# One tile for each quarter of w_in and w_out, and no dummy matmuls, in a fused gated-attention and MoE kernel

## The chip, the core and the metric

The kernel runs on one core of a Trainium2 chip. The metric is the device time in microseconds. A core has a matrix engine (TensorE, PE in the profile; its weight loads are PEld), a vector engine (VectorE, DVE), a scalar engine with function tables (ScalarE, ACT), a general engine (GpSimd, POOL) and SyncE (SP), which here only starts transfers. SP, ACT and POOL can each start DMA transfers; a transfer started by an engine stands in that engine's own order of instructions. Each engine runs its instructions in order; between engines semaphores order the work.

## What is computed

Four inputs of shape (batch 4, heads 8, sequence 768, head size 48) go through a recurrent attention; the result, as 3072 tokens of 384 numbers, goes through one feed-forward layer with w_in (384 x 2048) and w_out (2048 x 384).

```python
f = 1.0 / (1.0 + np.exp(-f_logit))
for t in range(S):
    state = f[:, :, t, :, None] * state + einsum('bhd,bhe->bhde', k[:, :, t], v[:, :, t])
    y[:, :, t] = einsum('bhd,bhde->bhe', q[:, :, t], state)
x = y.transpose(0, 2, 1, 3).reshape(B * S, H * D)
h = x @ w_in
out = (h * np.cos(h)) @ w_out
```

## The kernel before

**Tiling.** The 3072 tokens are 24 chunks of 128 (`C`), six for each batch. `chunk_load` (L391 to 402) fetches f, k, q and v of a chunk, four transfers of 192 KB, into one of seven sets of buffers. Which engine starts each transfer is in `QUEUES`, with one letter for each of f, k, q, v: chunk 0 "SAAP", chunk 1 "SSSS", chunk 2 "SSSA", so that chunk 2's v is started by ACT. `decay_group` (L404) makes the decay factors on ACT (exponential L412, logarithm L415, then L437 after a matmul). `attend` (L445) scales q and k (L458), casts v on POOL (L463), transposes (L481 on TensorE with L487 as the copy out, or a transposing DMA), forms the masked scores (L500, L507), carries the state (L519, L534, L538), makes y (L551, L554, L561) and its transpose x (L572, L561, tiles xT).

`moe` (L582) works on units of 128 or 256 tokens (`UNITS`). A unit's first half goes over groups of a PSUM bank: 12 matmuls (six in units of 256 tokens) of x with w_in (L597), the cosine on ACT (L605), the product on DVE (L609, tiles gT). Each group reads one quarter (512 columns) of w_in, and takes every fourth column of it, starting at f0. The second half (L619) multiplies gT by w_out, four matmuls for each quarter of w_out; the result is copied out (L628 or L630) and stored by SP (L633).

**Weights.** `load_weights` (L367) issues eight transfers from POOL, one for each quarter of w_in and of w_out, 384 KB each as written. Before the change w_in is one tile of 3 x 2048 columns and w_out one tile of 16 x 384; a quarter is a cut of that tile. A quarter of w_in is three pieces of 512 columns, 2048 apart; a quarter of w_out is contiguous. `GATES` holds each transfer back until the v of a given chunk is cast: 1, 1, 0, 1 for w_in and 1, 2, 2, 1 for w_out. So the third quarter of w_in (gate 0) is issued first, and the two middle quarters of w_out wait for chunk 2's v.

**Order.** All work is first written as operations with a cost, a priority and their dependences. A planner (`Plan.run`, L141) places them one by one: for each engine it computes the earliest start of every ready operation, with the ends of what it depends on, a free buffer, a free PSUM bank and a model of two DMA queues; it takes the operation of highest priority among those that can start soon, and where an operation may run on several engines, the one that would end first. The priorities come from lists of numbers (`ATT`, `DEC`, `MM1`, `MM2`). The result is a fixed order of instructions for each engine. The planner keeps its dependences by quarter of the weights. The semaphores are put in afterwards by the framework, from the address ranges that instructions read and write in a tile.

**Dummy matmuls.** `WARM` = 75 operations (L351 to 356) of two 128x128 matmuls of the identity with itself, of the lowest priority and in a PSUM bank that nobody reads. They are the 150 matmuls of L354. The planner gives each one 220 ns (the first 16) or 112 ns of TensorE.

The counters on which a transfer's end is seen are dealt in turn, eight for the transfers of SP and ACT together; a transfer whose counter is still in use waits for the one that used it.

Of the kernel before, what the change touches and what calls it, by code (L numbers as in the profile page):

```python
# [10 lines left out]
BF16 = mybir.dt.bfloat16  # L11
# [238 lines left out]
def kernel(  # L250
# [15 lines left out]
    d_model, d_ff = moe_w_in.shape  # L266
    n_tokens = B * S
    KM = d_model // 128
    KF = d_ff // 128
# [15 lines left out]
    QK_DMA = [7, 10, 12, 13, 14, 15, 16, 17, 18, 19, 20, 21, 22, 23]  # L285
    X_DMA = [7, 8, 11, 12, 13, 14, 16, 18, 19, 20, 21, 22, 23]
    FAST = 10
    WARM = 75
    BUFS = {"ld": 7, "vb": 6, "sp": 6, "b": 6, "bi": 4, "qk": 5, "qkt": 6, "am": 6, "sz": 4, "y": 4, "st": 2, "co": 5, "ot": 5, "g": 6}
    CAPS = [6, 4, 3, 3, 3]  # L290

    cpool = ctx.enter_context(tc.tile_pool(name="const", bufs=1))
# [42 lines left out]
    poS = Banks(base, "po", CAPS[2], [moe_cap])  # L335
    paS = Banks(base, "pa", CAPS[3])
    miS = Banks(base, "mi", CAPS[4])
    w_in_bf = cpool.tile([128, KM, d_ff], BF16, name="w_in_bf")
    w_out_bf = cpool.tile([128, KF, d_model], BF16, name="w_out_bf")

    P = Plan()

# [7 lines left out]
    warm = Val(phS)  # L350
    for i in range(WARM):  # L351
        def idle(e):
            for _ in range(2):
                nc.tensor.matmul(warm.ap[:, 0:128], lhsT=ident, rhs=ident, start=True, stop=True)  # L354
# [6 lines left out]


    NW = d_ff // 512
    w_in_v = [Val(ap=w_in_bf[:, :, i * 512:(i + 1) * 512]) for i in range(NW)]
    w_out_v = [Val(ap=w_out_bf[:, i * 4:(i + 1) * 4, :]) for i in range(KF // 4)]

    def load_weights(part, i, prio):  # L367
        if part == 0:
# [213 lines left out]
    def moe(u, t0, T):  # L582

        n0 = t0 // C
        xs, gT = xT[n0:(t0 + T) // C], Val(gS)
        x = x_sb[t0 // TOK][:, :, t0 % TOK:t0 % TOK + T]
        G = 512 // T
        span = T / C
        for j in range(KF // G):
            ph, co = Val(phS), Val(coS)  # L590

            def g1(e, j=j, ph=ph):
                for g in range(G):

                    s0, f0 = divmod(j * G + g, 4)
                    for m in range(KM):
                        nc.tensor.matmul(ph.ap[:, g * T:(g + 1) * T],  # L597
                                         lhsT=w_in_bf[:, m, s0 * 512 + f0:(s0 + 1) * 512:4],
                                         rhs=x[:, m, :],
                                         start=(g == 0 and m == 0),  # L600
                                         stop=(g == G - 1 and m == KM - 1))
            pr = MM1[u] + n0 + 0.5 * span * j * G / KF
            P.op({"PE": G * 3 * (T / 2.4 + 2.0)}, g1, reads=xs + [w_in_v[j * G // 4]],
                 writes=[ph], prio=pr, lat=170.0)
            P.op({"ACT": 490.0}, lambda e, ph=ph, co=co: nc.scalar.activation(  # L605
                out=co.ap, in_=ph.ap, func=AF.Sin, bias=HALF_PI),
                reads=[ph], writes=[co], prio=pr, table="S")
            gv = gT.part(lambda a, j=j: a[:, j * G:(j + 1) * G, 0:T])
            P.op({"DVE": 605.0}, lambda e, ph=ph, co=co, gv=gv: nc.vector.tensor_mul(  # L609
                out=gv.ap, in0=ph.ap.rearrange("p (g t) -> p g t", t=T),  # L610
                in1=co.ap.rearrange("p (g t) -> p g t", t=T)),
                reads=[ph, co], writes=[gv], prio=pr)
        for i in range(T // 128):
            po, ot = Val(poS), Val(otS)
            pr = MM2[u] + n0 + 0.5 * span + 0.5 * i
            for s in range(4):
                def g2(e, i=i, s=s, po=po):
                    for j in range(4 * s, 4 * s + 4):
                        nc.tensor.matmul(po.ap[:, 0:d_model],  # L619
                                         lhsT=gT.ap[:, j, i * 128:(i + 1) * 128],  # L620
                                         rhs=w_out_bf[:, j, :], start=(j == 0), stop=(j == KF - 1))
                P.op({"PE": 4 * 162.5}, g2,
                     reads=[gT.parts[q] for q in range(4 * s // G, (4 * s + 3) // G + 1)] + [w_out_v[s]],
                     writes=[po], prio=pr, lat=170.0 if s == 3 else 0.0)

            def ev(e, po=po, ot=ot):
                if e == "ACT":
                    nc.scalar.copy(out=ot.ap, in_=po.ap[:, 0:d_model])  # L628
                else:
                    nc.vector.tensor_copy(out=ot.ap, in_=po.ap[:, 0:d_model])  # L630
            P.op({"ACT": 375.0, "DVE": 475.0}, ev, reads=[po], writes=[ot], prio=pr)
            r0 = t0 + i * 128
            P.op({"SP": 500.0}, lambda e, ot=ot, r0=r0: nc.sync.dma_start(  # L633
                out=out[r0:r0 + 128, :], in_=ot.ap), reads=[ot], prio=pr, lat=1800.0, dma=500.0)
# [61 lines left out]
```

## Time and profile before

| | |
|---|---|
| median of 4 runs | 202.65 us (202.13 to 203.97) |
| profiled execution | 202.52 us |
| its span, first to last instruction | 200.6 us |
| granted TensorE clock, mean | 0.955 |
| PE busy | 179.4 us (89%), 2175 matmuls |
| DVE busy | 135.2 us (67%) |
| ACT busy | 138.2 us (69%) |
| POOL busy | 64.6 us (32%) |
| matmuls of L597 (x by w_in) | 864, 71.3 us |
| matmuls of L619 (gT by w_out) | 384, 71.2 us |
| dummy matmuls, L354 | 150, 12.5 us, from 1.4 to 26.5 us |
| transfers | 32.04 MB, mean 160 GB/s |

The profile is of one execution. A busy TensorE is not one at its peak, since matmuls overlap. In a line of the timeline the columns are: start, duration, engine, line of the kernel, operation, output and inputs, number of instructions, and in brackets the idle time before and what ended it. A line of the chain of waits has start, duration and what the chain went through. "SPq", "ACTq" and "POOLq" are an engine's issuing of transfers.

### The profile page before, as it was taken

How to read it: one execution, taken by the hardware profiler on the slowest of the kernel's cores; microseconds unless marked ns; L12 is line 12 of the kernel's file. 1: busy time of each engine (PE TensorE's matmuls, PEld its weight loads, DVE VectorE, ACT ScalarE, POOL GpSimd, SP SyncE). 2: the span in 40 equal slices, each digit the busy share in tenths (PEclk: the TensorE clock that was granted, in tenths of full speed). 3: DMA queues.
4: the chain of work that ended last, by engine and by line, in shares of the span. 5: the costliest groups of instructions: out<-in, count | busy, mean ns of one | idle time of the engine just before them, and what ended most of it. 6: DMA issues, size and time to landing. Idle time of an engine off the chain costs nothing.

```text
span 200.6 us, 5468 instructions
## 1 busy us (share of the span) xinstructions
PE 179.4 (89%) x2175; PEld 143.3 (71%) x2175; DVE 135.2 (67%) x254; ACT 138.2 (69%) x250; POOL 64.6 (32%) x105
## 2 busy tenths in 40 slices
PE   6891498299999999999999999889999999999991
PEld 6791397278766967998668785778678768697770
DVE  7592049376599999899757985569617984691630
ACT  4473026648598999999797469964879979193451
POOL 7290000360040213551786223911059257000000
PEclk9998569859999999999999999999999999999998
DMA  7999999992199798997999997999799954603003
GB/s 139 215 192 195 203 184 205 188 169 52 40 192 196 132 199 189 213 188 150 189 196 164 176 185 191 234 167 193 141 223 208 221 154 114 159 16 98 3 0 119
DMA packets 124713, 32.04 MB, mean 160 GB/s; under 512 B 119520, under 2 KB 124128, under 8 KB 124688
## 3 DMA queue, kind: packets, MB, share of 16 engines
q1 hardware_dynamic: 117248, 27.37, 68.4%
q0 software_dynamic: 2240, 3.34, 9.5%
q10 hardware_dynamic: 5200, 0.98, 2.6%
q8 instruction: 17, 0.28, 0.6%
q14 instruction: 8, 0.07, 0.1%
HBM read 25.17 MB, written 4.72 MB: 149 GB/s over the span
## 4 chain that ended last, share of the span: by engine, by line
PE 53%; SPq 14%; DMA 13%; DVE 9%; ACT 4%; issue 3%; POOL 2%; ACTq 0%; POOLq 0%; DVEq 0%
PE ps L597 23%; PE ps L619 20%; SPq L399 14%; DMA v<-in_v_dram 6%; DMA qkt<-qk 5%; DMA xT<-y 3%; DVE gT L609 3%; PE ps L500 3%; DVE am L507 2%; POOL qk L458 2%; DVE qk L458 2%; PE ps L551 1%; PE ps L427 1%; PE ps L519 1%; ACT cosh L605 1%
## 5 line engine op out<-in xcount | busy, mean ns | idle before, releaser
L597 PE MATMUL ps<-xT,w_in_bf 128*128 128x128 bf16 (+1 forms) x864 | 71.3, 243 | 8.4 <-DMA w_in_bf<-in_moe_w_in_dram 7.3
L597 PEld LDWEIGHTS <-w_in_bf 128*128 128x128 bf16 x864 | 66.8, 116 | 11.2 <-issue 5.2
L605 ACT ACTIVATE cosh<-ps 128x512 bf16<-128x512 f32 x96 | 54.4, 603 | 25.5 <-PE ps L597 21.2
L609 DVE TENSOR_TENSOR gT<-ps,cosh 128x512 bf16<-128x512 f32 x96 | 61.3, 686 | 15.6 <-ACT cosh L605 15.3
L619 PE MATMUL ps<-w_out_bf,gT 128*128 128x384 bf16 x384 | 71.2, 326 | 0.0
L619 PEld LDWEIGHTS <-gT 128*128 128x128 bf16 x384 | 34.5, 98 | 19.3 <-DVE gT L609 0.2
L507 DVE TENSOR_TENSOR am<-ps,umask 128x512 bf16<-128x512 f32 x48 | 30.5, 685 | 3.9 <-PE ps L500 3.7
L463 POOL CAST vb<-v 128x384 bf16<-128x384 f32 x24 | 12.1, 506 | 62.0 <-DMA v<-in_v_dram 52.4
L538 POOL TENSOR_TENSOR sz<-st,b 64x192 bf16<-64x192 f32 x32 | 16.6, 520 | 39.0 <-DVE st L534 30.9
L437 ACT ACTIVATE b<-ps 128x388 f32<-128x388 f32 x24 | 11.9, 497 | 11.6 <-PE ps L430 9.4
L534 DVE TENSOR_TENSOR st<-ps,sz 64x192 f32<-64x192 f32 x32 | 11.3, 354 | 9.0 <-PE ps L519 6.9
L561 ACT CAST y<-ps 128x384 bf16<-128x384 f32 x19 | 9.2, 482 | 10.1 <-PE ps L554 9.2
L458 POOL TENSOR_TENSOR qk<-q,b 128x384 bf16<-128x384 f32 x14 | 14.1, 1005 | 3.2 <-ACT b L437 2.5
L458 POOL TENSOR_TENSOR qk<-k,bi 128x384 bf16<-128x384 f32 x14 | 14.0, 1002 | 0.2
L354 PE MATMUL ps<-ident 128*128 128x128 bf16 x150 | 12.5, 245 | 1.4 <-POOL ident masks.py:199 1.4
L487 DVE COPY qkt<-ps 128x512 bf16<-128x512 bf16 x15 | 6.2, 422 | 10.8 <-PE ps L481 10.7
L412 ACT ACTIVATE f<-f 128x384 f32<-128x384 f32 x24 | 12.5, 522 | 1.0 <-DMA f<-in_f_logit_dram 0.9
L415 ACT ACTIVATE sp<-f 128x384 bf16<-128x384 f32 x24 | 12.6, 524 | 0.8
L630 DVE COPY ot<-ps 128x384 f32<-128x384 f32 x9 | 5.0, 556 | 10.2 <-PE ps L619 8.3
L437 ACT ACTIVATE bi<-ps 128x384 f32<-128x384 f32 x24 | 11.9, 495 | 0.0
L354 PEld LDWEIGHTS <-ident 128*128 128x128 bf16 x150 | 10.7, 112 | 1.6 <-POOL ident masks.py:199 1.4
L605 ACT ACT_TABLE_LOAD x9 | 11.5, 1283 | 0.2
(42 smaller groups left out, 153.7 us busy)
## 6 DMA issues: line engine op xcount, KB each, us to landing
f<-in_f_logit_dram SPq DMA_DIRECT2D x24, 192.0 KB, 4.0
out_dram<-ot SPq DMA_DIRECT2D x24, 192.0 KB, 2.3
k<-in_k_dram SPq DMA_DIRECT2D x23, 192.0 KB, 4.0
q<-in_q_dram SPq DMA_DIRECT2D x22, 192.0 KB, 3.8
v<-in_v_dram SPq DMA_DIRECT2D x21, 192.0 KB, 4.0
w_in_bf<-in_moe_w_in_dram POOLq DMA_DIRECT2D x4, 384.0 KB, 8.6
w_out_bf<-in_moe_w_out_dram POOLq DMA_DIRECT2D x4, 384.0 KB, 9.3
q<-in_q_dram ACTq DMA_DIRECT2D x2, 192.0 KB, 4.0
```

The lines of the kernel that those rows point to most:

```text
L354: nc.tensor.matmul(warm.ap[:, 0:128], lhsT=ident, rhs=ident, start=True, stop=True)
L399: P.op(eng, lambda e, t=t, ap=ap, dma=dma: dma.dma_start(out=t.ap, in_=ap), writes=[t], prio=prio, lat=3000.0 if way == "P" else 1250.0, d ...
L412: nc.scalar.activation(out=f.ap, in_=f.ap, func=AF.Exp, scale=-1.0)
L415: nc.scalar.activation(out=sp.ap[:, :, 0:D], in_=f.ap, func=AF.Ln, bias=1.0)
L437: nc.scalar.activation(out=o.ap, in_=pc.ap[:, 0:n], func=AF.Exp, scale=s)
L458: lambda e, src=src, w=w, dst=dst: E(e).tensor_mul(out=dst.ap, in0=src.ap, in1=w.ap[:, 0:H * D].rearrange("p (h d) -> p h d", d=D)),
L507: nc.vector.tensor_mul(out=am.ap, in0=pa.ap.rearrange("p (a n) -> p a n", n=C), in1=umask[:, None, :].broadcast_to([128, 4, C]))
L538: o = P.op(cost, lambda e, g=g, srcap=srcap, out=out: E(e).tensor_mul(out=out.ap, in0=srcap(), in1=bt.ap[rows(g), H * D:, None].broadcast_ ...
L597: nc.tensor.matmul(ph.ap[:, g * T:(g + 1) * T], lhsT=w_in_bf[:, m, s0 * 512 + f0:(s0 + 1) * 512:4], rhs=x[:, m, :], start=(g == 0 and m == 0),
L605: P.op({"ACT": 490.0}, lambda e, ph=ph, co=co: nc.scalar.activation(out=co.ap, in_=ph.ap, func=AF.Sin, bias=HALF_PI), reads=[ph], writes=[ ...
L609: P.op({"DVE": 605.0}, lambda e, ph=ph, co=co, gv=gv: nc.vector.tensor_mul(out=gv.ap, in0=ph.ap.rearrange("p (g t) -> p g t", t=T), in1=co ...
L619: nc.tensor.matmul(po.ap[:, 0:d_model], lhsT=gT.ap[:, j, i * 128:(i + 1) * 128], rhs=w_out_bf[:, j, :], start=(j == 0), stop=(j == KF - 1))
```

## The change

w_in becomes four tiles [128, 3, 512] and w_out four tiles [128, 4, 384]. The transfers, matmuls and their operands are otherwise the same: the same elements are loaded, and a weight load still takes every fourth column. `WARM` goes from 75 to 0, so the 75 dummy operations are not written, and the planner places the rest without them.

```diff
-    WARM = 75
+    WARM = 0
...
-    w_in_bf = cpool.tile([128, KM, d_ff], BF16, name="w_in_bf")
-    w_out_bf = cpool.tile([128, KF, d_model], BF16, name="w_out_bf")
+    w_in_bf = [cpool.tile([128, KM, 512], BF16, name=f"w_in_{i}") for i in range(d_ff // 512)]
+    w_out_bf = [cpool.tile([128, 4, d_model], BF16, name=f"w_out_{i}") for i in range(KF // 4)]
...
-    w_in_v = [Val(ap=w_in_bf[:, :, i * 512:(i + 1) * 512]) for i in range(NW)]
-    w_out_v = [Val(ap=w_out_bf[:, i * 4:(i + 1) * 4, :]) for i in range(KF // 4)]
+    w_in_v = [Val(ap=w_in_bf[i]) for i in range(NW)]
+    w_out_v = [Val(ap=w_out_bf[i]) for i in range(KF // 4)]
...
-                                         lhsT=w_in_bf[:, m, s0 * 512 + f0:(s0 + 1) * 512:4],
+                                         lhsT=w_in_bf[s0][:, m, f0::4],
...
-                                         rhs=w_out_bf[:, j, :], start=(j == 0), stop=(j == KF - 1))
+                                         rhs=w_out_bf[s][:, j - 4 * s, :], start=(j == 0), stop=(j == KF - 1))
```

## The prediction

> **What bounds the kernel now.** I read the page's slices first (its part 2), then the timeline of the first 60 us, then the chain of waits, then a table of stretches.
>
> ```profile
> PE   6891498299999999999999999889999999999991
> PEclk9998569859999999999999999999999999999998
> DMA  7999999992199798997999997999799954603003
> ```
>
> A slice is 5 us. From slice 8 on TensorE is busy nearly throughout. What is lost lies in the first 42 us and in slices 9 and 10, where the DMA engines are at 2 and 1 tenths.
>
> ```profile
> 0.00:16.00 16.00, 13.35 (x214) 12.14 (x214) 11.72 (x27) 8.49 (x17) 9.99 (x23) 1.00 1.09 183
> 16.00:30.00 14.00, 7.02 (x75) 6.68 (x76) 2.96 (x6) 3.25 (x5) 0.00 (x0) 0.63 1.10 194
> 30.00:42.00 12.00, 7.54 (x105) 6.32 (x103) 7.65 (x14) 7.82 (x15) 3.41 (x6) 0.88 0.99 188
> 42.00:60.00 18.00, 18.00 (x206) 13.86 (x204) 12.55 (x26) 13.12 (x21) 3.86 (x8) 0.89 0.55 109
> 60.00:100.00 40.00, 39.24 (x552) 31.76 (x550) 37.40 (x73) 36.79 (x70) 13.76 (x23) 1.00 0.92 183
> 100.00:150.00 50.00, 48.12 (x562) 36.97 (x558) 33.08 (x60) 37.28 (x71) 20.50 (x29) 1.00 0.98 186
> ```
>
> Columns: stretch, length, busy time of PE, weight loads, DVE, ACT and POOL, granted clock, DMA share, GB/s. Until 42 us the DMA engines are full (1.09, 1.10, 0.99) and TensorE is not. From 60 to 150 us both are (39.24 of 40 with 0.92; 48.12 of 50 with 0.98). So what brings the point near 42 us forward should bring the end forward by as much, if the loads come forward too.
>
> ```profile
> 15.75 0.48 ACT L561 CAST y<-ps 128x384 bf16<-128x384 f32 x1 [0.64 <-PE ps L554]
> 20.83 0.27 PE L597 MATMUL ps<-xT,w_in_bf 128*128 128x128 bf16 x1 [5.12 <-DMA w_in_bf<-in_moe_w_in_dram]
> 23.25 1.36 PE L597 MATMUL ps<-xT,w_in_bf 128*128 128x128 bf16 x11 [2.15 <-DMA w_in_bf<-in_moe_w_in_dram]
> 25.15 1.70 PE L354 MATMUL ps<-ident 128*128 128x128 bf16 x14
> 32.99 0.43 ACTq L399 DMA_DIRECT2D v<-in_v_dram  x1
> 54.66 0.36 SPq L633 DMA_DIRECT2D out_dram<-ot  x1
> ```
>
> The first 12 matmuls of a MoE group read one quarter of w_in, yet one ran at 20.83 and the other 11 at 23.25, each time just after a w_in transfer landed. The issue list, one issue at a time, gives issue and landing of the four quarters: 8.72 + 6.3 = 15.0; 10.54 + 7.7 = 18.2; 11.30 + 9.4 = 20.7; 12.07 + 11.1 = 23.2. So the first matmul waited for three quarters and the second for the fourth. A strided cut of one tile [128, 3, 2048] is taken as the whole address range from its first to its last element: row m=0 of a quarter touches few of these ranges, row m=1 all of them. The needed quarter is the one issued first: gate 0 is the third entry of GATES, the others have 1.
>
> ```profile
> 24.82 2.64 SPq L399
> 27.51 0.75 SPq L399
> 28.30 0.77 SPq L399
> 29.12 3.86 DMA v<-in_v_dram
> 32.99 4.79 DMA v<-in_v_dram
> 37.91 0.52 POOL vb L463
> 38.47 0.34 PE ps L519 x4
> ```
>
> The chain of waits does not pass through w_in. It runs down SP's loads to a v (chunk 4's) that lands at 32.98, and releases the v of chunk 2, which ACT issues at 32.99. That lands at 37.8; POOL casts it, then issues the last two quarters of w_out (38.4 and 41.3, each 6.2 us to landing). Those let the first output be made, whose store heads SP's queue until 54.66 and holds chunk 7's loads behind it: the dip in the DMA row. One v has nothing to give another as data. In the program of before, the hardware-queue transfers take eight completion counters in turn, and one that takes a counter waits until the transfer eight places ahead has landed. Chunk 2's v therefore has two conditions: ACT must have got past six cosines (the sixth ends at 31.92 + 0.60 = 32.52), and its counter must be free (32.98).
>
> **The change part by part.** The sum is against the profiled execution: 202.52 us, span 200.6, so 1.92 outside it; the median 202.65 is 0.13 above.
>
> w_out's tiles: nothing. Its quarters are contiguous, and 8 matmuls of L619 began at 33.06, before the last two quarters were issued; no wait across quarters exists there.
>
> w_in's tiles: the instructions are the same 864; a weight load still reads every fourth column, so I keep 113 ns. The first group can start when x of chunk 0 is there (13.46 + 0.46 = 13.9), its quarter has landed (15.0) and TensorE is free (15.7), so near 15.7 instead of 20.83/23.25. The sixth group needs the quarter of 20.7: two groups at the cold price (12 x 124 ns, from 1.36 us for 11) take 3.0, then 0.2 of hand-over and 0.60 of cosine: the sixth cosine ends near 24.5 instead of 32.52. That frees the first condition by 8 us. The second, 32.98, hides all of it unless it moves too.
>
> No dummy matmuls: 150 matmuls and 150 weight loads go. 136 of them (10.8 us of busy time) are before 16 us, in gaps; the last 14 stand at 25.15 to 26.85 ahead of ready transposes, about 1.5 us, hidden by the same load. Their effect on the end is indirect. They fill TensorE's program ahead of chunk 2's v, and the counters are dealt in the order in which the whole program is laid out. 150 at 56 to 113 ns is 8 to 17 us of TensorE's stream; only part of it is taken out of the order, since loads and ACT set much of it as well. I estimate that the v moves ahead of two to five of SP's loads, which follow each other about 1 us apart. Its counter partner is then not the v that landed at 32.98 but one of those landing at 32.2 (q, 28.30 + 3.9), 31.1 (k, 27.51 + 3.6), 30.0 (f, 24.82 + 5.2) or 29.3 (v, 19.30 + 10.0). I take 30.0: 3.0 us. The ends are 0 and 32.98 - 27.5 = 5.5 (a k load issued at 10.55, 17.0 to landing). An earlier v shares full DMA engines; I keep its own 4.79.
>
> What follows it moves by the same 3.0: on ACT two cosines, a table load and chunk 3's exponentials are queued behind that issue; on POOL the cast and two w_out issues; on TensorE L427 (37.06) and L519 (38.47). Next late would be w_out, 41.3 + 6.2 = 47.5, which moves with the cast; SP's store at 54.66 moves with it, and chunk 7's loads.
>
> The clock: the Trainium skill (TensorE: Matmul & The Clock Gate, section Why this matters for your kernels) says to warm up with at least 4 us of matmuls and to leave no gap over about 3 us, which speaks against dropping the dummies. The row: 1.00 in 0 to 16 us, but 0.63 in 16 to 30, where the 5 us gap undid the warming before the MoE began. Without dummies the real matmuls before 16 us run at half clock: the 13.35 us hold about 2.5 of real work, so by the rule up to 2.5 us more on TensorE. On chunk 0's path the transposes show the step, 0.40 to 0.63 us; six such steps make 1.4 us at most, x of chunk 0 at 15.3 instead of 13.9, still about where the quarter lands (15.0) and before TensorE is free (15.7). By the trace 0; by the rule up to 2.5 if that cover were gone. I take 0.
>
> The planner's own order: 75 operations leave its books, each one 112 or 220 ns of its time, and the bank that they held. It picks engines, banks and order by earliest start, so anything may flip. No row shows this. A gain: real operations no longer planned behind a filler, at most the 1.5 us above. A loss: a load or store put further back; five places of 1.0 us, the distance of the landings above, is 5. I take 0 and keep -1.5 and +5.
>
> Sum: 202.65 - 3.0 = 199.65, rounded to **199.6 us**.
>
> **The rivals.** (1) Hidden: chunk 2's v keeps its partner at 32.98. Then ACT merely waits there earlier, everything after is as before, and the time is 202.4 (202.0 to 203.2). For it: the condition is in the trace. Against: so much is removed from the layout in front of that load. 0.2.
>
> (2) Slower: the new order puts a chunk's load behind something late, as SP's store at 54.66 does now, for which SP stood idle 16.6 us. The place is SP's queue before its first store, or chunk 2's v on ACT. The price is about 1 us for each place that the v moves back, or for each load (0.8 to 1.2 us of issue) that falls behind the store; from two places on it is over 1%. Three to five places give 205 to 207. For it: the engine that issues a load is fixed by a list, and so is its place against that engine's other work once the order is made. Against: up to 42 us full DMA engines set the order, and the dummies did not slow these. 0.28.
>
> (3) More: the partner's landing is 28 or earlier and w_out comes earlier than its cast alone would bring it, 5 to 7 us, 196 to 197.5. The DMA engines are full until 42 us, which speaks against it. 0.07. The forecast itself (1.5 to 5 us) has 0.45.
>
> **How the numbers follow.** About 1% is what a measurement of this kernel tells from no change. Faster by over 1% (under 200.6): 0.42 of the forecast's 0.45, rival 3's 0.07, and 0.03 of rival 1 with a small gain from a flip: 0.52. Within 1%: the rest of rival 1 (0.17) and the forecast's weak end (0.03), 0.20. Slower: rival 2, 0.28. The forecast's own range is 197.5 to 201. For 8 in 10 it reaches down to 195.5 and up to 205.5, which leaves out about half of rival 2 and the far end of rival 3.
>
> **What would show it.** Right: the first L597 near 15.7 with 12 together; the fourth quarter waited for only by its own group; chunk 2's v issued by ACT at 28 to 31; POOL's cast at 33 to 36; SP's first store near 51. The clock low before 16 us with no later start of the MoE for it. Wrong: the v still at 33; or the dip of slices 9 and 10 longer; or an idle TensorE after 60 us that was not there.

## The result, and the profile after

| | before | after |
|---|---|---|
| median | 202.57 us (199.77 to 204.69, 56 runs) | 200.72 us (199.35 to 203.5, 35 runs) |
| profiled execution | 202.52 us, span 200.6 | 201.15 us, span 198.8 |
| after against before, in turn on one chip | | 0.9944 [0.9924, 0.9964] |
| a second comparison (experiment 5) | 200.94 us | 199.46 us, 0.9923 [0.989, 0.9955] |

The change gains 0.56% (1.1 us) in the first comparison and 0.77% (1.5 us) in the second. Both intervals lie below 1; the gains are a third and a half of the 3.0 us that the prediction summed. A ratio compares only runs within 1.5% of the fastest of their kernel, so it is not the quotient of the two medians (0.991), and the profiles of experiments 2 and 11 are of runs that it leaves out. Line numbers are one higher than before from L340 on (an edited kernel shifts them further by the lines of its edit): the loads are L400, POOL's cast L464, x by w_in L598, the cosine L606, gT by w_out L620, the store L634.

The timeline of after:

```profile
15.62 1.48 PE L598 MATMUL ps<-xT,w_in 128*128 128x128 bf16 x12
22.39 2.61 ACT L606 ACTIVATE cosh<-ps 128x512 bf16<-128x512 f32 x4 [1.23 <-DVE gT L610]
31.25 0.38 ACTq L400 DMA_DIRECT2D v<-in_v_dram  x1
31.73 1.09 ACT L606 ACTIVATE cosh<-ps 128x512 bf16<-128x512 f32 x2 [6.74 <-DMA k<-in_k_dram]
35.25 0.48 PE L428 MATMUL ps<-sp,umask 128*128 128x384 bf16 x1 [8.25 <-ACT sp L416]
35.51 0.51 POOL L464 CAST vb<-v 128x384 bf16<-128x384 f32 x1 [18.77 <-DMA v<-in_v_dram]
51.89 0.36 SPq L634 DMA_DIRECT2D out_dram<-ot  x1
```

The first group of 12 runs at 15.62, all 12 together; before, one ran at 20.83 and eleven at 23.25. The sixth cosine ends at 22.39 + 2.61 = 25.0, 7.5 us earlier. But ACT then stands idle for 6.74 us in front of chunk 2's v, until a k lands. The v goes out at 31.25, only 1.74 us earlier than the 32.99 of before. POOL's cast starts 2.4 us earlier (37.91 before), SP's first store 2.8 us (54.66 before).

The chain of waits of after, in a window from the start to 60 us:

```profile
27.41 3.82 DMA k<-in_k_dram
31.25 4.13 DMA v<-in_v_dram
...
35.51 0.52 POOL vb L464
36.07 0.48 PE ps L520 x4
```

The form is that of before: after SP's loads, one load with nothing to give chunk 2's v, that v, POOL, TensorE. What changed is the load in the first line: chunk 4's k, landing at 27.41 + 3.82 = 31.23, in place of chunk 4's v, landing at 32.98. The trace also records the counter on which each transfer signals: SP's and ACT's transfers use eight numbers (100, 102 to 106, 108, 109) in turn. Chunk 2's v has 102 in before, which chunk 4's v took eight transfers ahead of it; in after it has 109, which chunk 4's k took eight ahead. On that number the v waits.

The page's slices of after (40 slices of the span, in tenths), and three stretches (columns as in the table of stretches above):

```profile
PE   0578940799999999999999999999999699999991
PEclk9999997579999999999999999999999999999999
DMA  7999999992598997898999798989599756603003
```

```profile
16.00:30.00 14.00, 10.21 (x122) 8.88 (x120) 6.74 (x13) 5.20 (x8) 0.57 (x2) 1.00 1.14 200
30.00:42.00 12.00, 5.85 (x63) 4.58 (x63) 4.96 (x11) 6.31 (x11) 4.92 (x9) 0.60 1.09 203
42.00:60.00 18.00, 17.67 (x215) 13.11 (x213) 14.09 (x28) 14.79 (x24) 2.66 (x5) 0.98 0.62 125
```

TensorE does 10.21 us of work in 16 to 30 (7.02 before), then runs dry: it is idle from about 27 to 35.25, and in 30 to 42 the granted clock is 0.60 (0.88 before, where the stretch at half clock comes later, as shown below under the clock). The false wait is gone, and one for the v stands in its place. There is also a new 6 among the nines of the PE row, in slice 31 (counted from 0, as in the prediction); it is taken up below, where the gain is followed to the end.

Leaving out the dummies, SP and POOL run the same operations in the same order as before, by the names of their tiles. ACT hands one copy (L487 before) to DVE, and the orders of TensorE and DVE differ within the first chunks only (in the first 24 us of after). Later shifts are shifts in time, not in order.

### The profile page after: what moved, and what is told of

Read it like the earlier page. It is cut to its first block, busy times and chain, and to the rows that moved or that the text cites. A ratio compares the mean times of both kernels' runs of the same rounds, so it can differ in the third digit from the quotient of the medians.

```text
span 198.8 us, 5167 instructions
## 1 busy us (share of the span) xinstructions
PE 172.7 (87%) x2025; PEld 135.2 (68%) x2025; DVE 135.1 (68%) x255; ACT 137.8 (69%) x249; POOL 64.7 (33%) x105
## 4 chain that ended last, share of the span: by engine, by line
PE 48%; SPq 16%; DMA 14%; DVE 9%; ACT 7%; issue 2%; POOL 1%; POOLq 0%; DVEq 0%; ACTq 0%
PE ps L598 21%; PE ps L620 18%; SPq L400 15%; DMA v<-in_v_dram 5%; DMA xT<-y 4%; DVE gT L610 4%; PE ps L501 2%; DMA k<-in_k_dram 2%; DMA q<-in_q_dram 2%; DMA qkt<-qk 2%; PE ps L520 1%; PE ps L552 1%; ACT f L413 1%; DVE am L508 1%; PE ps L482 1%
## 5 line engine op out<-in xcount | busy, mean ns | idle before, releaser
L598 PE MATMUL ps<-xT,w_in 128*128 128x128 bf16 (+1 forms) x864 | 71.1, 243 | 0.6 <-DMA xT<-y 0.6
L606 ACT ACTIVATE cosh<-ps 128x512 bf16<-128x512 f32 x96 | 54.5, 603 | 24.7 <-PE ps L598 8.6
L620 PE MATMUL ps<-w_out,gT 128*128 128x384 bf16 x384 | 71.2, 326 | 0.0
L598 PEld LDWEIGHTS <-w_in 128*128 128x128 bf16 x864 | 66.8, 116 | 3.1 <-issue 1.0
L620 PEld LDWEIGHTS <-gT 128*128 128x128 bf16 x384 | 34.5, 98 | 19.3 <-DVE gT L610 0.2
L464 POOL CAST vb<-v 128x384 bf16<-128x384 f32 x24 | 12.1, 506 | 59.8 <-DMA v<-in_v_dram 48.0
L428 PE MATMUL ps<-sp,umask 128*128 128x384 bf16 x24 | 8.6, 362 | 13.7 <-ACT sp L416 13.6
L431 PEld LDWEIGHTS <-sp 128*128 128x128 bf16 x96 | 6.2, 101 | 14.7 <-issue 12.7
L501 PE MATMUL ps<-qkt 48*128 48x128 bf16 x192 | 10.4, 233 | 2.4 <-DMA qkt<-qk 1.8
```

The lines of the kernel that those rows point to most:

```text
L501: nc.tensor.matmul(pas[g].ap[:, p * C:(p + 1) * C], lhsT=kdt.ap[64 * g:64 * g + D, p, :], rhs=qdt.ap[64 * g:64 * g + D, p, :], start=(p == ...
L598: nc.tensor.matmul(ph.ap[:, g * T:(g + 1) * T], lhsT=w_in_bf[s0][:, m, f0::4], rhs=x[:, m, :], start=(g == 0 and m == 0), stop=(g == G - 1 ...
L620: nc.tensor.matmul(po.ap[:, 0:d_model], lhsT=gT.ap[:, j, i * 128:(i + 1) * 128], rhs=w_out_bf[s][:, j - 4 * s, :], start=(j == 0), stop=(j ...
```

## Experiments

Ratios are against runs of before on the same chip. The starting point is marked: edits of "after" or of "before".

**1 and 2. The two halves of the change alone.** After with the dummies put back, and before without its dummies:

```diff
  (1, of after)
-    WARM = 0
+    WARM = 75
  (2, of before)
-    WARM = 75
+    WARM = 0
```

> The tiles of the change, with the 75 dummy operations kept. Theory (chunk 2's v is held by its counter, and only the layout without the dummies gives it an earlier partner): the first L598 group starts near 15.7 to 16.5 and the sixth cosine ends near 25, but ACT issues chunk 2's v at 33.0 as in the kernel before, POOL casts it near 37.9, the first store goes at 54 to 55; time 202.6, ratio to before 0.998 to 1.002. Rival (the earlier start of the MoE is itself what gains): 200.7 to 201.5, ratio 0.991 to 0.995.

> No dummy operations, with w_in and w_out one tile each. Theory: the first group still starts at 20.8/23.2; without the 14 dummies the sixth cosine ends near 31, and the counter's partner is the q that landed at 32.2, so chunk 2's v is issued at 32.2, cast near 36.8, 1 us before the kernel before and 1.3 us after the changed kernel; time 201.8 to 202.3, ratio 0.996 to 0.999. Rival (removing the dummies alone is the whole gain): cast near 35.5, time 200.7 to 201.5, ratio 0.991 to 0.995.

Measured: the tiles alone 0.9999 [0.9974, 1.0024]; the missing dummies alone 0.9958 [0.9925, 0.999]. The timeline of the tiles alone:

```profile
15.63 0.83 PE L598 MATMUL ps<-xT,w_in 128*128 128x128 bf16 x12
22.49 1.94 ACT L606 ACTIVATE cosh<-ps 128x512 bf16<-128x512 f32 x3 [0.53 <-PE ps L598]
34.21 0.39 ACTq L400 DMA_DIRECT2D v<-in_v_dram  x1
34.70 1.09 ACT L606 ACTIVATE cosh<-ps 128x512 bf16<-128x512 f32 x2 [10.28 <-DMA v<-in_v_dram]
54.48 0.36 SPq L634 DMA_DIRECT2D out_dram<-ot  x1
```

The sixth cosine ends at 24.4, and ACT then waits 10.28 us for chunk 4's v, which in this profile lands 1.2 us later than in before. Eight microseconds of removed wait are worth nothing that the ratio can tell, because this load stands behind them. Without dummies and with the old tiles, the partner is chunk 4's q, the v goes out at 32.81, while ACT is at its fifth and sixth cosine (32.13 to 33.40), so the late cosines now hold it, and the store starts at 53.91. For the start the halves do not add: alone they issue the v at 34.21 and 32.81, together at 31.25 (32.99 before), since each condition hides what the other half sets free. The times are too close to tell it: 0.9999 x 0.9958 = 0.9957, inside the interval of the whole change.

**3. The hiding load taken out of the way.** Of after: chunk 2's v is moved in the order ahead of chunk 3's f, so ACT issues it before the cosines.

```diff
+    v2 = loads[2, 3]
+    order.remove(v2)
+    order.insert(order.index(loads[3, 0]), v2)
```

> The changed kernel, with the load of chunk 2's v put on ACT ahead of the first cosine; all else in the same order. Theory: it is issued at 16.5, lands by 26, chunk 3's L428 moves from 35.3 to about 29 to 30, the first store from 51.9 to 46 to 48. If the start is carried to the end in full, 195 to 196.5 us (ratio to before 0.965 to 0.97); if only in the share of the changed kernel's profile (1.8 of 2.8 us), 197 to 198.5 (0.975 to 0.98). Rival (the middle is bound by the stream of loads alone, and the start is worth nothing): 200.7.

Measured: 0.9559 [0.9506, 0.9613], 193.37 us. ACT issues the v at 15.82. Its timeline and clock row:

```profile
22.46 4.02 ACT L608 ACTIVATE cosh<-ps 128x512 bf16<-128x512 f32 x6 [1.34 <-PE ps L600]
28.90 0.51 POOL L466 CAST vb<-v 128x384 bf16<-128x384 f32 x1 [12.19 <-DMA v<-in_v_dram]
28.92 0.32 PE L430 MATMUL ps<-sp,umask 128*128 128x384 bf16 x1 [1.12 <-ACT sp L418]
43.76 0.36 SPq L636 DMA_DIRECT2D out_dram<-ot  x1
```

```profile
PEclk9999999999999999999999999999999999999999
```

Six cosines now follow one another with no load between them, TensorE starts chunk 3 at 28.92 instead of 35.25, its clock never drops, and the first store comes 10.9 us earlier than before. That is more than either forecast. Part of it is the v's own early landing; experiments 10 and 11 set the part of the tiles apart.

**4. The first store moved behind chunk 7's loads.** Of after: SP's first store goes behind chunk 7's k, q and v, which it holds back.

```diff
+    first = [o for o in order if o in stores.values()][0]
+    order.remove(first)
+    order.insert(order.index(loads[7, 3]) + 1, first)
```

> The changed kernel, with SP's first store put behind the k, q and v of chunk 7. Theory that the stretch from 55 to 150 us is bound by the stream of loads: these three go out at 37 to 40 instead of 52.3 to 54.4, the rest of the loads comes about 2 us earlier, the last v at 147 to 148 instead of 149.3; 198.5 to 199.5 us, ratio 0.98 to 0.987. Rival (TensorE's own order binds there, loads are early enough): the loads move and the time doesn't, 200.5 to 201, ratio 0.991 to 0.996.

Measured: 0.9907 [0.9874, 0.9939], 199.57 us. The dip shrinks (DMA share 0.76 in 42 to 60, after 0.62) and the last load of the inputs is issued at 146.60, after 149.33, but the ratio is only 0.0016 to 0.0037 under those of after (0.9923 and 0.9944), and the intervals overlap. The loads moved, and a gain is not shown: this is closer to the rival than to the theory.

**5 and 9. The two kernels again, for the spread of profiles.** No edit.

> The changed kernel once more, for a second profile beside kernels of the same chip. Theory: the start repeats (ACT issues chunk 2's v at 31 to 31.5, POOL casts it at 35.3 to 35.8, first store at 51.5 to 52.3), the time around the span is 2.3 to 2.5 us against 2.0 of the kernel before, ratio 0.990 to 0.996. Rival (the start's gain differs from one execution to the next, so that 2.4 us in one profile was luck): cast anywhere from 35.5 to 37.9.

> The kernel before once more, for a second profile of it. Theory (its start is always the same, the rest of the span varies from one execution to the next): POOL casts chunk 2's v at 37.2 to 38.2, first store at 53.8 to 55, span 198 to 201, ratio 0.998 to 1.002. Rival (the first profile's start was a late one): cast at 36.5 or earlier, which would make the changed kernel's gain at the start smaller than 2.4.

Measured: after 0.9923 [0.989, 0.9955]; before against itself 1.0031 [1.0006, 1.0056], so about 0.3% is the least that a ratio here can tell. The starts repeat: the second profile of after has the v at 31.34, the cast at 35.21 and the store at 50.98, the second of before the cast at 37.72 and the store at 54.51. What follows does not repeat. Taken at the same matmuls of gT by w_out, the two profiles of before stay within 0.2 us until 104 us, and then the second runs ahead: 0.8 us at 121, 3.1 at the end (span 197.4 against 200.6).

**6 and 7. A few dummies put back.** Of after, 4 or 28 matmuls of the identity in front of chunk 0's L428:

```diff
-            def pe(e, pc=pc, sp=sp):
+            def pe(e, pc=pc, sp=sp, warm=28 if (b, c) == (0, 0) else 0):
+                for _ in range(warm):
+                    nc.tensor.matmul(pc.ap[:, 0:128], lhsT=ident, rhs=ident, start=True, stop=True)
```

> The changed kernel with four dummy matmuls ahead of chunk 0's first matmul (so TensorE works at 1.4 us instead of 5.3); the counter's partner of chunk 2's v stays the same. Theory (the 0.4 us outside the span comes of TensorE starting late): around the span 2.0, time 0.3 to 0.4 us less than the changed kernel. Rival (it comes of something else that the 150 dummies did): around the span 2.4 and no difference.

> The changed kernel with 28 dummy matmuls ahead of chunk 0's first matmul, in the 3.9 us in which TensorE waits there. The compiled program then gives chunk 2's v the partner that it had before the change (chunk 4's v). Theory: ACT issues it at 32.8 to 33.5, cast at 37.2 to 38, first store at 53.7 to 54.8, and the gain is gone: ratio to before 0.998 to 1.002. Rival (the layout doesn't matter, the dummies' work or the false waits did): cast 35.5 and ratio 0.990 to 0.995 as the changed kernel.

Measured: 4 dummies 0.9932 [0.9907, 0.9958], as after; 28 dummies 1.005 [1.0025, 1.0075], somewhat above the forecast. The timeline with 28:

```profile
23.47 1.53 PE L600 MATMUL ps<-xT,w_in 128*128 128x128 bf16 x24 [0.61 <-DMA w_in<-in_moe_w_in_dram]
33.31 0.42 ACTq L400 DMA_DIRECT2D v<-in_v_dram  x1
33.83 1.08 ACT L608 ACTIVATE cosh<-ps 128x512 bf16<-128x512 f32 x2 [10.33 <-DMA v<-in_v_dram]
53.98 0.36 SPq L636 DMA_DIRECT2D out_dram<-ot  x1
```

With 28 the partner is chunk 4's v again (counter 102, as in before; with 4, and with the 130 later ones of experiment 8, it is 109, as in after), the store is back at 53.98 and the gain is gone. The MoE does not start later for it: the first L600 stands at 15.62, as in after. So matmuls laid out ahead of the v decide which load it waits for. Why this kernel is 1.0 us slower than before, with a store 0.7 us earlier, was not followed. The first line shows the fourth quarter of w_in waited for 0.61 us, by its own groups alone.

**8. Dummies in the gap.** Of after, the same edit with 130 matmuls in front of chunk 3's L428 (`warm=130 if (b, c) == (0, 3)`), which run from 27.26 to 34.7.

> The changed kernel with 130 dummy matmuls in the gap from 27.0 to 35.2 us, ahead of chunk 3's L428. Theory (the half clock from 35 to 43 us is on the path): granted clock 1.0 from 35 to 43, L598's groups there at 0.7 instead of 1.3 us, the first store 1.5 to 2.5 us before 51.9, time 1 to 2 us under the changed kernel, ratio to before 0.981 to 0.988. Rival (DVE, ACT, POOL and w_out's landing near 45.2 hold that stretch, TensorE doesn't): clock 1.0 and no gain, ratio 0.990 to 0.996.

Measured: 0.9882 [0.983, 0.9934], 197.96 us, the lowest time of the kernels that keep the load where it is. Its stretch, its partner and its store; below, the second profile of after, which is of the same chip:

```profile
30.00:42.00 12.00, 9.14 (x163) 8.30 (x161) 5.85 (x12) 7.14 (x13) 4.79 (x9) 1.00 1.08 196
```

```profile
32.56 1.09 ACT L608 ACTIVATE cosh<-ps 128x512 bf16<-128x512 f32 x2 [7.14 <-DMA k<-in_k_dram]
36.11 0.51 POOL L466 CAST vb<-v 128x384 bf16<-128x384 f32 x1 [19.45 <-DMA v<-in_v_dram]
39.62 0.85 PE L600 MATMUL ps<-xT,w_in 128*128 128x128 bf16 x12
50.71 0.36 SPq L636 DMA_DIRECT2D out_dram<-ot  x1
```

```profile
30.00:42.00 12.00, 6.01 (x74) 5.00 (x74) 5.39 (x12) 6.87 (x13) 4.92 (x9) 0.57 1.16 211
```

```profile
35.21 0.51 POOL L464 CAST vb<-v 128x384 bf16<-128x384 f32 x1 [18.34 <-DMA v<-in_v_dram]
39.19 1.48 PE L598 MATMUL ps<-xT,w_in 128*128 128x128 bf16 x12
50.98 0.36 SPq L634 DMA_DIRECT2D out_dram<-ot  x1
```

The cast is 0.9 us later, and yet the store is 0.3 earlier. In between, the clock is 1.00 instead of 0.57, and 12 matmuls take 0.85 us instead of 1.48. By this one pair of profiles the half clock after the gap costs about 1.2 us at this place: 0.9 made up and 0.3 gained. The timed difference, 0.9923 to 0.9882, is 0.8 us, with intervals that overlap.

**10, 11 and 12. The load given to another queue.** Chunk 2's v is issued by POOL's queue instead of ACT's, at the place of experiment 3. Edits of before (10), of after (11), and of after with `WARM = 75` (12):

```diff
+            if (b, c, len(vals)) == (0, 2, 3):
+                dma = nc.gpsimd
...
+    v2 = loads[2, 3]
+    order.remove(v2)
+    order.insert(order.index(loads[3, 0]), v2)
```

> The kernel before (one tile each, 75 dummy operations), with chunk 2's v issued by POOL behind the first six weight transfers, so that neither ACT's place nor a counter of SP's and ACT's holds it. Theory: it lands near 29, but the false waits now show: cosines seven and eight end near 33 to 34, chunk 3's L427 is at 35.5 to 36.5, first store at 52.5 to 54; ratio 0.991 to 0.998. Rival (the false waits are worth nothing anywhere): start as in the next kernel, ratio near 0.96.

> The changed kernel with chunk 2's v issued by POOL behind the first six weight transfers. Theory (with the v out of the way, the tiles' earlier MoE shows): chunk 3's L428 at 29 to 31, first store at 44 to 47, ratio 0.955 to 0.97. Rival (only the v's own time counts, the tiles nothing): as the kernel before with the same v, 0.991 to 0.998.

> The tiles of the change with the 75 dummy operations, and chunk 2's v issued by POOL as in the two kernels beside it. Theory (with no counter to be dealt, the dummies matter little: 14 of them cost at most 1.5 us of TensorE near 17 to 20, and they keep the clock up before 16): within 0.005 of the ratio of the changed kernel with the same v, 0.955 to 0.972. Rival (the dummies themselves cost time): 0.98 or more.

Measured: 0.9799 [0.9716, 0.9882] for before so changed, 0.9517 [0.9462, 0.9572] for after, 0.9527 [0.9477, 0.9577] for the tiles with dummies (190.94 us). The timelines of 10 and of 12:

```profile
21.02 0.27 PE L601 MATMUL ps<-xT,w_in_bf 128*128 128x128 bf16 x1 [5.48 <-DMA w_in_bf<-in_moe_w_in_dram]
23.36 1.36 PE L601 MATMUL ps<-xT,w_in_bf 128*128 128x128 bf16 x11 [2.07 <-DMA w_in_bf<-in_moe_w_in_dram]
36.19 0.32 PE L431 MATMUL ps<-sp,umask 128*128 128x384 bf16 x1 [1.77 <-ACT sp L419]
51.82 0.36 SPq L637 DMA_DIRECT2D out_dram<-ot  x1
```

```profile
17.19 0.83 PE L602 MATMUL ps<-xT,w_in 128*128 128x128 bf16 x12
28.50 0.32 PE L432 MATMUL ps<-sp,umask 128*128 128x384 bf16 x1 [0.98 <-ACT sp L420]
45.79 0.36 SPq L638 DMA_DIRECT2D out_dram<-ot  x1
```

In 10 the v is cast at 28.40, but the false waits of the first group stand, and chunk 3 begins at 36.19 behind the late cosines. In 12 it begins at 28.50. With the v out of the way the tiles are worth 0.9517 / 0.9799 = 0.971, some 6 us, and the dummies nothing that these runs can tell (0.9517 and 0.9527). The ratio of experiment 10 is the least certain: two of its six runs carry it, and the median of all six, 198.09 us, is only 1.7 us under before's 199.80, within what was expected. From that median to the 191.51 of experiment 11 the tiles are worth 6.6 us, so their gain does not hang on it. Both 11 and 12 are faster than before and after, by a little more than was forecast.

## Why the prediction was half right

**The bound and the hiding: right.** The first group came at 15.62 (forecast near 15.7), the sixth cosine ended at 25.0 (24.5), and all of it was hidden by chunk 2's second condition. That was argued from one line of the chain; the experiments show it: the tiles alone give 0.9999 with the load in its place, and with it moved they are worth 0.971 (11 against 10).

**"No dummies: counters are dealt differently": right in kind, too large in size.** The forecast was a shift by two to five places, taken as three (f, landing at 30.0). It was two: k, whose landing at 31.23 is the 31.1 that the prediction listed. (Its list does not quite fit its words: it begins one place away, with q, and the k of its far end, issued at 10.55, is six away.) So the v went out at 31.25, 1.7 us earlier and not 3.0, and since it then took 4.13 us instead of the 4.79 that I kept, it landed 2.4 us earlier. Of the term of 3.0, 0.6 was never there. The counters in the traces and experiment 7 show the mechanism.

**The failed step: "what brings the point near 42 us forward should bring the end forward by as much".** The 3.0 was carried to the end whole. The runs say otherwise. In us against before; the first store is from one profile of each kernel, the time is what the ratio makes of before's median of its batch, with intervals of 0.4 us either way for after to 1.7 for 10:

| kernel | first store | time |
|---|---|---|
| 1, tiles alone | -0.2 | 0.0 |
| 2, no dummies alone | -0.8 | -0.8 |
| 9, before again | -0.2 | +0.6 |
| 7, 28 dummies | -0.7 | +1.0 |
| after | -2.8 | -1.1 |
| 5, after again | -3.7 | -1.6 |
| 6, 4 dummies | -2.7 | -1.4 |
| 4, store late | -3.7 (store moved) | -1.9 |
| 8, dummies in the gap | -4.0 | -2.4 |
| 3, v early | -10.9 | -8.9 |
| 10, before, v by POOL | -2.8 | -4.0 |
| 11, v by POOL | -8.7 | -9.7 |
| 12, the same with dummies | -8.9 | -9.5 |

In after, in both comparisons, and in 3, 6, 7 and 8 some 1 to 2 us of the gain at the start are missing at the end. In 10, 11 and 12 the time gains more than the store shows, by no more than the intervals. Two pieces of the loss can be named. First, the time outside the span was taken as a constant 1.92. It is not: its median is 2.00 to 2.03 in the kernels that have the scattered dummies, and 2.37 to 2.47 in those that do not. That is 0.4 us of loss which no view of the span shows. Second, TensorE waits once more late in the span. The wait, and the chain of waits of after that leads to it:

```profile
158.97 0.40 PE L501 MATMUL ps<-qkt 48*128 48x128 bf16 x8 [1.78 <-DMA qkt<-qk]
```

```profile
153.55 2.02 SPq L634
...
155.67 3.25 DMA qkt<-qk
...
158.97 0.40 PE ps L501 x8
```

A transposing transfer that TensorE needs stands behind stores on SP's queue, and TensorE waits 1.78 us for it: that is the 6 in slice 31. The second profile of after has the same wait, 1.17 us long (the 7 in slice 31 of its PE row, below). Its chain comes there another way: a v load that lands at 146.8, POOL's scaling, and a transpose that takes from 150.69 to 156.06.

```profile
PE   0587960699999999999999999999999799999991
```

The same eight matmuls wait 0.8 to 1.0 us in experiments 2, 4, 6 and 8, less in 3 and 12 (0.25 and 0.48), and not at all in the two profiles of before and in 1, 7, 10 and 11. At the same matmuls after is 2.4 to 2.8 us ahead of before from 48 to 125 us and 4.0 near 149, but 1.4 at 162 and 1.8 at the end; from second profile to second it is 3.5 ahead until 119 us, and 1.5 from 162 on. The condition "if the loads come forward too" held only in part: the last load of the inputs is issued 1.9 us earlier (149.33, before 151.23) where the first store was 2.8 earlier, and 2.3 from second profile to second, where the store was 3.5 earlier.

Counted from the cast, 0.6 (partner) + 0.4 (outside the span) of the missing 1.5 to 1.9 us have a name. The wait at L501 is large enough for the other 0.5 to 0.9. That it is just this wait is not shown, since the two profiles of before alone part by 3.1 us between 104 us and the end, and why 7 and 11, which have no scattered dummies either, are without it stays open. That full DMA engines are behind it is argued from their share (0.92 to 1.06 in 60 to 150 us in the two profiles each of before and after); experiment 4 does not bear it out.

The median of 200.72 lies in the forecast's range of 197.5 to 201. That confirms nothing: by the ratio the change is worth 1.1 us, which would be 201.5 from the 202.65 of the forecast.

**The clock, taken as 0: right at the place weighed.** By the rule on warming, up to 2.5 us were at stake before 16 us. Nothing of that came: without the dummies the first 12 matmuls took 1.48 us instead of 0.83 (experiment 1), but started at the same 15.6. The clock row does not show this slow pace: it has 1.00 in 0 to 16 us in after too, so only the durations tell. What I did not weigh is the other half of the same rule (the Trainium skill, TensorE: Matmul & The Clock Gate, section Why this matters for your kernels), which warns of gaps, at chunk 3. There the half clock costs about 1.2 us at the store and 0.8 in the time, by experiment 8, whose interval overlaps with that of after. But the change did not bring it. Before runs chunk 3 at half clock too, after idle times of 2.53 and 1.02 us where after has 8.25. Two stretches of before, and its group of 12 there:

```profile
40.00:42.00 2.00, 1.66 (x18) 1.39 (x16) 1.62 (x4) 1.28 (x4) 1.78 (x4) 0.50 0.93 144
42.00:44.00 2.00, 2.00 (x22) 1.44 (x20) 0.96 (x4) 0.33 (x1) 1.30 (x3) 0.50 1.02 186
```

```profile
41.74 1.48 PE L597 MATMUL ps<-xT,w_in_bf 128*128 128x128 bf16 x12
```

**The planner's order, taken as 0: right.** Rival 2, slower by two or more places in SP's queue, did not happen: SP's order is the same. Rival 1 (hidden, 202.4) is what the tiles alone do (0.9999). Rival 3 did not happen with the change alone; experiments 3, 11 and 12 show what it would have needed, the v off its place.

## What to carry to other kernels

Before sizing a removed wait, look for the next condition behind the same instruction: here an engine waited for nothing in the data, only for a transfer's completion counter, and 8 us of removed wait were worth nothing until the one load that used it was issued early or from another queue (0.956 and 0.952). Carry a gain at the start to the end with a discount where TensorE and DMA are both full, and do not read that region from one pair of profiles. The scattered dummies ahead of the first groups were worth nothing that shows (11 and 12); those that filled the gap ahead of chunk 3 kept the clock up for the work behind it (8), with a gain in time that is not clear of the noise. Adding or dropping them can move counters that loads wait on.

## What was unexpected of the hardware

- Twenty-eight matmuls that nobody reads, all ahead of chunk 0's first matmul, cost some 2.5 us (1.005 against 0.9923), through the completion counter of one load. Four cost nothing that shows (0.9932).
- The time around the span depends on the program: 2.0 us with 150 scattered dummies, 2.4 without. Starting TensorE earlier with 4 dummies did not bring it back (2.41), nor did 130 later ones (2.46). The cause stays open.
- After about 8 us of an idle TensorE the granted clock stayed at half for some 6 us of work, back-to-back groups of 12 matmuls among it (experiment 5: 0.50 in 35 to 39 us, 0.55 in 39 to 41, 1.00 from there). In before it stayed at half for some 6 us after idle times of 2.53 and 1.02 us (0.50 in 40 to 44, 1.00 from 46).
